# A fused attention and expert kernel: another order of loads, dots, far sums and turnings where its dense phase hands over to its expert phase

## The chip, the cores and the metric

One core of one Trainium2 chip runs the kernel in one launch. The metric is device time in microseconds (us): the median of 3 runs is 1411.21 us before the change (1410.98 to 1413.54). TensorE multiplies, VectorE and ScalarE do arithmetic on tiles, GpSimd (POOL) does some arithmetic and issues indirect DMAs, and SyncE (SP) issues most DMAs. Each engine works through its own queue in order and waits there for semaphores.

## The reference

All in float32, 4608 tokens of 512 elements:

```
kv = einsum('bhsd,bhse->bhde', k, v);  out = einsum('bhsd,bhde->bhse', q, kv)
x  = out / sqrt(mean(out*out, -1) + 1e-6) * g_norm        # 8 heads of 64 side by side: 512
h  = x @ w_in;  x = (max(h,0) + alpha*min(h,0)) @ w_out   # dense block, 512 -> 2048 -> 512
logits = x @ w_gate + modality_bias[modality_id]          # 8 experts
e_idx = argmax(logits);  gate_w = softmax(logits)[e_idx]
out[e_idx == e] = gate_w * (max(x[e_idx == e] @ w1[e], 0) @ w2[e])   # 512 -> 1024 -> 512
```

## The kernel before, in words

**First phase.** Twelve chunks (c) of 384 tokens. For each the attention of the next chunk is made beside the dense block of this one, which runs over 16 blocks (s) of 128 hidden elements: `first` (12 matmuls), then `second` (9 matmuls) of the block before. Numbers are split into a high and a low fp32r part, so each product is three matmuls. The dense weights lie in the tile `W`, 2048 columns per block. When a chunk is done, `y_out` copies its three tiles of 128 tokens (t) out of PSUM, `dots` makes the 24 logit columns per tile on VectorE, `choose`, `weigh`, `count` and `place` give expert, gate and a place in a bucket of that expert, and `scatter` writes the rows to the buffer `xb` in HBM. Beside this SyncE moves the experts' weights, split in parts, to `wsp` in HBM.

**Second phase.** 41 tiles (i) of 128 rows, each of one expert, sorted by expert; two slots in `W`, each with the 8 MB of one expert in two halves of 4 MB: the first half for `layer1` (24 matmuls), the second for `layer2` (24 matmuls). The expert with the most rows so far (the leader) comes first, since its first tiles are full before the last chunk is routed. Per tile: `load_rows` reads the rows from `xb` (four DMAs and a small one for gate and token number), `turn_rows` turns them and splits them (xhi, xlo), `layer1` with a ReLU (hh), `turn_h` turns and splits the result (hth, htl), `layer2` into PSUM (y2), a scaling and an indirect DMA to the output. Tiles 0 to 2 (`i < PLAIN`) are turned by TensorE through PSUM (4 transposes for rows, 8 for hh) and evicted by ScalarE and VectorE; later ones are turned by VectorE.

**Change of phase.** While the last chunk is still to be routed, TensorE already works on tiles 0 and 1 of the leader. The logits of the last chunk are divided: `dots` 0 to 7 and 16 to 21 (tiles t = 0 and 2 of the chunk, read straight from PSUM) on VectorE, and ten far ones, `far_mul` on GpSimd and `far_add` (a sum along the row) on ScalarE through two buffers. After `place`, `padding` writes eight blocks of empty rows (the ends of the buckets) to `xb`, `table` makes the lists that say which tile belongs to which expert, and from tile 4 on rows come from these lists.

**What sets the order.** It is written out by hand (`manual_schedule`): each engine gets its instructions in the order of the code, and semaphores are put between them. SyncE's DMAs take eight semaphores in turn; a DMA whose semaphore still belongs to one that has not landed waits for it. In `load_expert` SyncE waits for each half to land (L591) before its next instruction; and the first half of expert 0 and of expert 1 waits until the rows loaded last have landed (L589). PSUM tiles `y` (three banks) serve the last chunk's sums, then `turned` and y2; the pools opened at L941 to L943 take over the other banks. Two engines that read one PSUM bank are put one behind the other: `y_out(c, 0)` on ScalarE waits for the `dots` of that bank.

Of the kernel before, what the change touches and what calls it, by code (L numbers as in the profile page):

```python
# [8 lines left out]
F32 = mybir.dt.float32  # L9
# [5 lines left out]
ALU = mybir.AluOpType  # L15
# [4 lines left out]
NTOK = 4608  # L20
D = 512
S = 576
E = 8
# [4 lines left out]
BUCKET = 4736  # L28
NIT = 43
MAIN = 41  # L30
# [14 lines left out]
def fused(ctx: ExitStack, tc, qT, kv, g2, wmoe, alpha, wgate, bias, modality, w12, out):  # L45
# [58 lines left out]
    def other(n=512):  # L104
        return (pools[1] if pools else ps_a).tile([128, n], F32, tag="a", name="a")
# [289 lines left out]
    def y_out(c, t):  # L395
        if t == 1:
            lg_t[c] = one.tile([128, 3, E], F32, tag="lg", name="lg")
            yb_t[c] = [three.tile([128, ROW], F32, tag="yrow", name="yrow") for _ in range(3)]
        y = yb_t[c][t][:, 0:D]
        if t == 0 and c < NCH - 1:  # L400
            V.tensor_copy(y, y_t[c][t])
        else:
            A.copy(y, y_t[c][t])

    def dots(c, lo, hi):
        for i in range(lo, hi):
            t, e = divmod(i, E)
            y = y_t[c][t] if c == NCH - 1 else yb_t[c][t][:, 0:D]
            V.tensor_tensor_reduce(junk, y, wg_sb[:, e, :], 1.0, 0.0, ALU.mult, ALU.add, lg_t[c][:, t, e:e + 1])  # L409
# [72 lines left out]
    def padding():  # L482

        pi = one.tile([1, E], I32, name="pi")
        V.tensor_copy(pi, base[0:1, :])
        for e in range(E):
            r = SP.value_load(pi[0:1, e:e + 1], min_val=e * BUCKET, max_val=e * BUCKET + NTOK)
            i = SP.dma_start(xb[ds(r, 128)], pad)
            tc.declare_no_dep(i.ins, group="rows", reason="rows that no token has")
            if e:  # L490
                tc.declare_no_dep(i.ins, group="pads", reason="rows apart")
            tc.add_to_no_dep_group("pads", i.ins)
# [18 lines left out]
    def table():  # L511
# [62 lines left out]
        V.tensor_copy(ts[:, 1, :], ids[:, 0:E])  # L574
        yield

    def load_expert(j, halves=(0, 1)):
        tab = tab_0[0:1, 0:1] if j == 0 else tab_sp[0:1, E + j:E + j + 1]
        eid = SP.value_load(tab, min_val=0, max_val=E - 1)
        if j:  # L580
            thr = SP.value_load(tab_sp[0:1, j:j + 1], min_val=1, max_val=MAIN + 1)
        for half in halves:
            if j:
                SP.wait_ge(sem_2 if half else sem_1, thr)
            o = half * (SLOT // 2)
            at = (j & 1) * SLOT + o
            d = SP.dma_start(W[:, at:at + SLOT // 2].bitcast(F32), wsp[ds(eid, 1), :, o:o + SLOT // 2].rearrange("a p c -> p (a c)"))
            tc.add_to_no_dep_group("experts", d.ins)
            if j < 2 and half == 0:  # L589
                tc.add_manual_dep(d.ins, row_dma[0], data, reason="the first rows go first")  # L590
            s = SP.sem_inc(sem_w, 1)  # L591
            tc.add_manual_dep(s.ins, d.ins.name, data, reason="the weights are in")


    rows, x2, hh, ht, regs, row_dma = {}, {}, {}, {}, {}, []
# [19 lines left out]

    order = lambda t: t.rearrange("p (c a j) -> p c a j", c=4, a=4)

    def turned(x):
        ps = ps_y.tile([128, D], F32, tag="y", name="turned") if pools else other()
        for k in range(4):  # L620
            PE.transpose(ps[:, k * 128:(k + 1) * 128], x[:, k * 128:(k + 1) * 128], ident)
        return ps

    def turn_rows(i):

        x = rows.pop(i)
        o = (i % 3) * 512
        hi = xhi.rearrange("p a b -> p (a b)")[:, o:o + 512]
        lo = xlo.rearrange("p a b -> p (a b)")[:, o:o + 512]
        flat = x.rearrange("p a b -> p (a b)")  # L630
        if i < PLAIN:
            ps = turned(flat)
            A.copy(hi, ps)
            V.tensor_tensor(lo, ps, hi.bitcast(F32), ALU.subtract)
            x2[i] = hi, lo
            return
        V.transpose(flat, flat)
        x = x.rearrange("p a (c j) -> p c a j", c=4)
        A.copy(order(hi), x)
        V.tensor_tensor(order(lo), x, order(hi).bitcast(F32), ALU.subtract)  # L640
        x2[i] = hi, lo
# [114 lines left out]
    with tc.manual_schedule():  # L756
# [74 lines left out]
        for c in range(NCH):  # L831
# [3 lines left out]
            for s in range(NFB):  # L835
# [61 lines left out]
                if c > 0:  # L897
                    if s < 8:
                        dots(c - 1, 3 * s, 3 * s + 3)
                    if s == 7:  # L900
                        choose(c - 1)
                    if s == 8:
                        count(c - 1)
                        weigh(c - 1)
                    if s == 9:
                        place(c - 1)
                        if nxt == NCH:
                            leader()
                            scatter(c - 1, range(3))
                    if nxt < NCH and 9 <= s < 12:  # L910
                        scatter(c - 1, [s - 9])
                    if nxt == NCH and s == 11:
                        for i in range(3):
                            load_rows(i)
                        load_expert(0)
                elif edge:
                    pre_load(0)
                    SP.dma_start(wg_sb.rearrange("p a b -> p (a b)"), wgate.rearrange("a b -> (a b)").partition_broadcast(128))
                    G.memset(pad, 0.0)
                    G.memset(pad[:, D + 1:D + 2].bitcast(I32), OOB)  # L920
                    for j in range(8):
                        SP.dma_start(xb[E * BUCKET + j * 128:E * BUCKET + (j + 1) * 128], pad)
# [22 lines left out]
        add = lambda *js: [far_add(c, j) for j in js]  # L945
        far_mul(c, 0)
        far_mul(c, 1)
        add(0)
        dots(c, 0, 4)
        layer1(0, lambda: add(1, 2))  # L950
        turn_rows(2)
        load_rows(3)
        dots(c, 4, 8)
        y_out(c, 0)
        add(3, 4)
        layer1(1, lambda: add(5, 6))
        turn_h(0)
        dots(c, 16, 22)
        add(7, 8, 9)
        choose(c)  # L960
        weigh(c)
        layer2(0, lambda: count(c))
        place(c)
        scatter(c, range(3))
        padding()
        steps = table()
        next(steps)
        turn_h(1)
        next(steps)
        load_rows(4)  # L970
        load_rows(5)
        next(steps)
        for j in range(1, E):
            load_expert(j)
        for i in range(2, MAIN):
            if PLAIN < i + 1 < MAIN:
                turn_rows(i + 1)
            layer1(i)
            if i + 1 == PLAIN:
                turn_rows(i + 1)  # L980
            if 2 < i < MAIN - 3:
                load_rows(i + 3)
            if i == 3:
                _, words[:] = nc.values_load_multi_w_load_instructions(
                    tab_pe[0:1, 0:6], engines=[PE.engine], min_val=0, max_val=8 ** 8 - 1)
            if i == 8:
                items = nc.values_load(tab_pe[0:1, 6:7], min_val=0, max_val=NIT)
            layer2(i - 1)
            turn_h(i)
# [52 lines left out]
```

## Time and profile before

| | |
|---|---|
| median of 3 runs | 1411.21 us (1410.98 to 1413.54) |
| the profiled execution | 1413.03 us, of which the span is 1411.4 us |
| busy in the span | TensorE matmul 1365.8 us (97%), VectorE 1033.0 (73%), GpSimd 654.5 (46%), ScalarE 524.6 (37%) |
| granted TensorE clock, mean | 0.992 |

The span is what the engines' records cover; 1.6 us of the execution lie outside it. Times in the rows are us from the span's start. The first phase ends on TensorE at about 930 us; all of the change lies between about 911 us and 990 us.

### The profile page before, as it was taken

To read this page: it belongs to the slowest core of one execution; us is meant where nothing else is said; L and a number is where in the kernel's file an instruction comes from. 1 tells how busy PE (TensorE), PEld (TensorE's weight loads), DVE (VectorE), ACT (ScalarE), POOL (GpSimd) and SP (SyncE) were. 2 spreads that over 40 slices of the span, in tenths; PEclk is the share of its full clock that TensorE was granted. 3 is DMA by queue.
4 is the path that set the end of the run, shared out by engine and by line. 5 is a ranking of instruction groups with operands and counts; after the bars stand their busy time and mean duration, and the time that the engine had idled before them with its cause. 6 is when DMAs were issued, how large, how long until landed. Compare 5 with 4: busy or idle time off the path is not lost. (4 is left out here: it accounts for less than half of the span.)

```text
span 1411.4 us, 26831 instructions
## 1 busy us (share of the span) xinstructions
PE 1365.8 (97%) x8886; PEld 1160.9 (82%) x8886; DVE 1033.0 (73%) x2247; ACT 524.6 (37%) x1136; POOL 654.5 (46%) x641
## 2 busy tenths in 40 slices
PE   8889999999999999999999999979999999999997
PEld 7778888788888888888888888867888888888886
DVE  6999887777877687967887888737666666666663
ACT  4673323232322323232323232133445544445442
POOL 2665645455645464645555564532333333333321
PEclk9999999999999999999999999999999999999999
DMA  8854645454545554455645252464711161537784
GB/s 281 273 195 135 212 138 191 144 192 134 180 168 191 169 190 158 157 191 168 214 141 200 91 194 84 153 256 135 275 53 48 46 269 58 194 142 286 296 327 177
DMA packets 88950, 250.71 MB, mean 178 GB/s; under 512 B 19245, under 2 KB 39213, under 8 KB 86640
## 3 DMA queue, kind: packets, MB, share of 16 engines
q1 hardware_dynamic: 77056, 220.83, 45.0%
q0 software_dynamic: 11760, 28.14, 6.1%
q8 instruction: 78, 1.28, 0.4%
q14 instruction: 56, 0.46, 0.1%
HBM read 158.69 MB, written 91.54 MB: 177 GB/s over the span
## 5 line engine op out<-in xcount | busy, mean ns | idle before, releaser
L361 PE MATMUL h<-xhi,W 128*128 128x384 f32 x1536 | 429.7, 340 | 1.3 <-POOL W L185 0.7
L375 POOL TENSOR_TENSOR glo<-gg,ghi 128x384 fp32r<-128x384 f32 x192 | 225.8, 1177 | 388.7 <-ACT ghi L373 366.7
L389 PE MATMUL y<-W,ghi 128*128 128x512 f32 x1152 | 307.9, 402 | 24.1 <-ACT ghi L373 22.4
L361 PEld LDWEIGHTS h<-xhi,W 128*128 128x128 f32 x1536 | 281.7, 188 | 12.1 <-ACT xhi L350 1.4
L389 PEld LDWEIGHTS y<-W,ghi 128*128 128x128 f32 x1152 | 211.7, 189 | 74.9 <-ACT ghi L373 37.6
L361 PE MATMUL h<-xlo,W 128*128 128x384 f32 x768 | 259.3, 338 | 0.0
L409 DVE CUSTOM_DVE_ANT_0 junk<-yrow,wg_sb 128x512 f32<-128x512 f32 x264 | 244.4, 926 | 6.7
L645 PE MATMUL h<-W,xhi 128*128 (+1 forms) x656 | 207.5, 397 | 4.0 <-DMA W<-wsp 4.0
L645 PE MATMUL y<-W,hth 128*128 (+1 forms) x656 | 205.0, 394 | 5.4 <-DVE htl L697 5.0
L373 ACT CAST ghi<-gg 128x384 fp32r<-128x384 f32 x192 | 98.2, 512 | 267.9 <-DVE gg L369 201.0
L215 POOL TENSOR_TENSOR raw<-raw 128x512 f32<-128x512 f32 x128 | 197.1, 1540 | 0.5
L368 DVE TENSOR_SCALAR gg<-h,alpha_sb 128x384 f32<-128x384 f32 x176 | 107.5, 611 | 115.6 <-PE h L361 112.1
L211 ACT CAST raw<-raw 128x512 fp32r<-128x512 f32 x128 | 79.6, 622 | 279.2 <-DMA raw<-in_w_dram 166.2
L722 POOL DMA_INDIRECT out_dram<-kvbd,tail x41 | 43.6, 1063 | 282.6 <-ACT kvbd L720 240.9
L389 PE MATMUL y<-W,glo 128*128 128x512 f32 x576 | 168.4, 401 | 0.0
L645 PEld LDWEIGHTS y<-W,hth 128*128 128x128 f32 x656 | 124.2, 190 | 34.2 <-DVE htl L697 5.3
L645 PEld LDWEIGHTS h<-W,xhi 128*128 128x128 f32 x656 | 123.7, 189 | 34.0 <-DVE lg L409 4.3
L361 PEld LDWEIGHTS h<-xlo,W 128*128 128x128 f32 x768 | 144.2, 188 | 6.9 <-DVE xlo L351 0.2
L389 PEld LDWEIGHTS y<-W,glo 128*128 128x128 f32 x576 | 107.4, 190 | 30.9 <-POOL glo L375 6.3
L645 PE MATMUL y<-W,htl 128*128 (+1 forms) x328 | 130.4, 398 | 0.0
L645 PE MATMUL h<-W,xlo 128*128 (+1 forms) x328 | 130.1, 397 | 0.0
L682 DVE TENSOR_SCALAR hh<-h 32x256 f32<-32x256 f32 x296 | 123.3, 416 | 4.6
(204 smaller groups left out, 1469.5 us busy)
## 6 DMA issues: line engine op xcount, KB each, us to landing
wsp<-raw SPq DMA_DIRECT2D x128, 512.0 KB
W<-wsp SPq DMA_DIRECT2D x16, 4096.0 KB
raw<-in_w_dram SPq DMA_DIRECT2D x128, 256.0 KB
kvt<-in_kv_dram SPq DMA_DIRECT2D x30, 512.0 KB
xs<-xb POOLq DMA_DIRECT2D x140, 64.0 KB
raw<-in_wmoe_dram SPq DMA_DIRECT2D x17, 512.0 KB
qT<-in_qT_dram SPq DMA_DIRECT2D x11, 768.0 KB
wg_sb<-in_wmoe_dram SPq DMA_DIRECT2D x15, 512.0 KB
```

What stands on the lines that cost most here:

```text
L211: A.copy(sp_t[n][:, 0:512].bitcast(F32R), sp_t[n][:, 512:1024])
L215: G.tensor_tensor(lo, lo, hi, ALU.subtract)
L361: PE.matmul(ps, w_at(fb, part)[:, k * 128:(k + 1) * 128], x[:, k, :], start=(i == 0), stop=(i == 11))
L368: V.tensor_scalar(gg, ps, 0.0, alpha_sb[:, fb:fb + 1], ALU.min, ALU.mult)
L373: A.copy(ghi, gg)
L375: G.tensor_tensor(glo, gg, ghi.bitcast(F32), ALU.subtract)
L389: PE.matmul(y_t[c][t], a[:, t * 128:(t + 1) * 128], w, start=(fb == i == 0), stop=(fb == NFB - 1 and i == 2))
L409: V.tensor_tensor_reduce(junk, y, wg_sb[:, e, :], 1.0, 0.0, ALU.mult, ALU.add, lg_t[c][:, t, e:e + 1])
L645: m = PE.matmul(ps, a, w, start=start, stop=stop)
L682: m = V.tensor_scalar(to, of, 0.0, None, ALU.max) if mine else A.activation(to, of, AF.Relu)
L722: d = G.indirect_dma_start(out=out, out_offset=IndirectOffsetOnAxis(ap=tail[:, i, 1:2].bitcast(I32), axis=0), in_=y, in_offset=None, bound ...
```

## The change

At block s = 11 of the last chunk SyncE's queue gets the rows of tile 0, the first half of the leader's weights, the rows of tiles 1 and 2, then the second half. SyncE no longer waits behind the first half of expert 0: its semaphore for both is counted up after the second. The wait for the rows loaded last (L589) stays for expert 1 only. The transposes of tile 1 go to the PSUM bank `spare`. `dots` 0 to 7 come in one run ahead of `layer1(0)`, four far sums between the halves of `layer1(0)`, then `y_out(c, 0)`, which stood behind the second half of the dots. `turn_h(0)` moves into `layer1(1)`, between its two halves of 12 matmuls; `turn_h(1)` goes ahead of the scatter and the tables; `turn_rows(3)` ahead of the last part of the tables; `turn_h(2)` into `layer2(1)`, behind its 18th matmul. `padding` loads the eight ends into registers with one load ahead of the eight writes.

On SyncE, from the rows of tile 2 to the rows of tile 3, before (`xs` are rows, `tail` the small DMA, TENSOR_LOAD and ISA fetch an address; each waits for the semaphores named):

```order
L614 DMA tail<-xb 128x2 [waits DMAHW0_49]
L579 TENSOR_LOAD tab_111
L579 ISA x2
L587 ISA
L587 DMA W<-wsp 128x8192 [waits DMAHW7_49,DMAHW1_49,PE_49]
L587 ISA [waits DMAHW1_49]
L587 DMA W<-wsp 128x8192 [waits DMAHW2_49,PE_49]
L604 TENSOR_LOAD tab_111 [waits DMAHW2_49]
```

Now, from the rows of tile 0 into the rows of tile 1, and then from the rows of tile 2 on:

```order
L623 DMA tail<-xb 128x2 [waits DMAHW6_49]
L584 TENSOR_LOAD tab_111
L584 ISA x2
L592 ISA
L592 DMA W<-wsp 128x8192 [waits DMAHW1_49,DMAHW7_49,DMAHW0_49,PE_49]
L613 TENSOR_LOAD tab_111
L613 ISA x2
L621 ISA
L621 DMA xs<-xb 128x4x32
```

```order
L621 DMA xs<-xb 128x4x32 [waits DMAHW7_49]
L621 ISA
L621 DMA xs<-xb 128x4x32 [waits DMAHW0_49]
L623 ISA
L623 DMA tail<-xb 128x2 [waits DMAHW1_49]
L584 TENSOR_LOAD tab_111
L584 ISA x2
L592 ISA
L592 DMA W<-wsp 128x8192 [waits DMAHW2_49,PE_49]
L613 TENSOR_LOAD tab_111 [waits DMAHW7_49,DMAHW2_49]
```

The first half stands two tiles of rows earlier; the third piece of rows of tile 2 now waits for its landing (semaphore DMAHW7), the second half waits for the third piece of tile 1's rows (DMAHW2), and the wait for both halves stands ahead of the rows of tile 3.

On TensorE, around the end of `layer1(1)` (h_9889), before:

```order
L645 MATMUL h_9889<-W,xhi 128x512 x2
L645 MATMUL h_9889<-W,xlo 128x512
L621 MATMUL turned<-ident,hh 128x128 x8
L645 MATMUL y_9972<-W,hth 128x512 x2
L645 MATMUL y_9972<-W,htl 128x512
```

and now, in the middle of `layer1(1)` (h_9901) and on to `layer2(0)` (y_9980):

```order
L654 MATMUL h_9901<-W,xlo 128x512
L630 MATMUL turned<-ident,hh 128x128 x8
L654 MATMUL h_9901<-W,xhi 128x512 x2
L654 MATMUL h_9901<-W,xlo 128x512
L654 MATMUL h_9901<-W,xhi 128x512 x2
L654 MATMUL h_9901<-W,xlo 128x512
L654 MATMUL h_9901<-W,xhi 128x512 x2
L654 MATMUL h_9901<-W,xlo 128x512
L654 MATMUL h_9901<-W,xhi 128x512 x2
L654 MATMUL h_9901<-W,xlo 128x512
L654 MATMUL y_9980<-W,hth 128x512 x2
```

The eight transposes of tile 0's hidden rows no longer stand directly ahead of `layer2(0)`: twelve matmuls of `layer1(1)` lie between.

On ScalarE, from the last far sum ahead of `layer1(0)`'s ReLU on (kvbd are the far products, hh the ReLUs, hth the turned and rounded result), before:

```order
L418 ACTIVATE kvbd_100,lg<-kvbd_100 128x512
L677 ACTIVATE hh<-h_9826 128x4x4x32 x2
L633 CAST xhi<-turned 128x512
L403 COPY yrow<-y 128x512
L418 ACTIVATE kvbd_101,lg<-kvbd_101 128x512
L418 ACTIVATE kvbd_100,lg<-kvbd_100 128x512
L418 ACTIVATE kvbd_101,lg<-kvbd_101 128x512
L418 ACTIVATE kvbd_100,lg<-kvbd_100 128x512
L677 ACTIVATE hh<-h_9889 128x4x4x32 x2
L696 CAST hth<-turned 128x512 x2
```

and now:

```order
L418 ACTIVATE kvbd_101,lg<-kvbd_101 128x512
L686 ACTIVATE hh<-h_9836 128x4x4x32 x2
L403 COPY yrow<-y 128x512
L642 CAST xhi<-turned 128x512
L418 ACTIVATE kvbd_100,lg<-kvbd_100 128x512
L418 ACTIVATE kvbd_101,lg<-kvbd_101 128x512
L705 CAST hth<-turned 128x512 x2
L418 ACTIVATE kvbd_100,lg<-kvbd_100 128x512
L418 ACTIVATE kvbd_101,lg<-kvbd_101 128x512
L686 ACTIVATE hh<-h_9901 128x4x4x32 x2
```

Two far sums, not four and a ReLU, stand between the rounding of tile 2's rows (xhi) and that of tile 0's hidden rows (hth).

The diff, cut to its core:

```diff
         V.tensor_copy(pi, base[0:1, :])
+        _, ends = nc.values_load_multi_w_load_instructions(pi, engines=[SP.engine], min_val=0, max_val=E * BUCKET)
         for e in range(E):
-            r = SP.value_load(pi[0:1, e:e + 1], min_val=e * BUCKET, max_val=e * BUCKET + NTOK)
+            r = SP.alloc_register(f"end{e}")
+            SP.reg_alu(r, ends[e], 0, ALU.add)
+            r = SP.snap(r, min_val=e * BUCKET, max_val=e * BUCKET + NTOK)
...
-            if j < 2 and half == 0:
+            if j == 1 and half == 0:
                 tc.add_manual_dep(d.ins, row_dma[0], data, reason="the first rows go first")
-            s = SP.sem_inc(sem_w, 1)
-            tc.add_manual_dep(s.ins, d.ins.name, data, reason="the weights are in")
+            landed.append(d.ins.name)
+            if j == half == 0:
+                continue
+            while landed:
+                s = SP.sem_inc(sem_w, 1)
+                tc.add_manual_dep(s.ins, landed.pop(0), data, reason="the weights are in")
...
-            ps = turned(flat)
+            ps = turned(flat, None if pools else spare if i else other())
...
-                        for i in range(3):
-                            load_rows(i)
-                        load_expert(0)
+                        load_rows(0)
+                        load_expert(0, (0,))
+                        load_rows(1)
+                        load_rows(2)
+                        load_expert(0, (1,))
...
-        add(0)
-        dots(c, 0, 4)
-        layer1(0, lambda: add(1, 2))
+        dots(c, 0, 8)
+        layer1(0, lambda: add(0, 1, 2, 3))
+        y_out(c, 0)
         turn_rows(2)
         load_rows(3)
-        dots(c, 4, 8)
-        y_out(c, 0)
-        add(3, 4)
-        layer1(1, lambda: add(5, 6))
-        turn_h(0)
-        dots(c, 16, 22)
-        add(7, 8, 9)
+        dots(c, 16, 18)
+        add(4, 5)
+        layer1(1, lambda: [turn_h(0), add(6, 7)])
+        dots(c, 18, 22)
+        add(8, 9)
         choose(c)
         weigh(c)
-        layer2(0, lambda: count(c))
+        layer2(0)
+        count(c)
         place(c)
+        turn_h(1)
         scatter(c, range(3))
         padding()
         steps = table()
         next(steps)
-        turn_h(1)
         next(steps)
         load_rows(4)
         load_rows(5)
+        layer1(2)
+        turn_rows(3)
         next(steps)
         for j in range(1, E):
             load_expert(j)
-        for i in range(2, MAIN):
-            if PLAIN < i + 1 < MAIN:
+        layer2(1, lambda: turn_h(2))
+        for i in range(PLAIN, MAIN):
+            if i + 1 < MAIN:
                 turn_rows(i + 1)
             layer1(i)
-            if i + 1 == PLAIN:
-                turn_rows(i + 1)
```

## Rows read from the trace of the kernel before

**Rows 1.** The page, part 1: busy us, share of the span, instructions.
```profile
PE 1365.8 (97%) x8886; PEld 1160.9 (82%) x8886; DVE 1033.0 (73%) x2247; ACT 524.6 (37%) x1136; POOL 654.5 (46%) x641
```
**Rows 2.** Windows: us, busy by engine, granted clock, DMA share, GB/s.
```profile
115.50:123.50 8.00, 8.00 (x43) 7.46 (x43) 6.46 (x14) 2.63 (x5) 1.68 (x2) 1.00 1.02 294
...
915.60:918.60 3.00, 3.00 (x18) 2.78 (x17) 0.88 (x2) 0.00 (x0) 0.81 (x1) 1.00 0.68 91
...
954.50:960.00 5.50, 5.50 (x13) 4.35 (x14) 5.12 (x16) 1.60 (x6) 1.29 (x1) 0.50 0.00 0
...
970.00:1380.00 410.00, 410.00 (x1780) 333.29 (x1779) 271.44 (x528) 199.63 (x439) 137.99 (x212) 1.00 0.51 183
```
**Rows 3.** Timeline of TensorE: start, us, line, out<-in, idle before and its releaser.
```profile
930.49 0.60 PE L621 MATMUL a<-ident,xs 128*128 128x128 f32 x4
935.13 0.70 PE L645 MATMUL h<-W,xhi 128*128 128x512 f32 x2 [4.05 <-DMA W<-wsp]
...
942.35 0.60 PE L621 MATMUL turned<-ident,xs 128*128 128x128 f32 x4
942.71 0.71 PE L645 MATMUL h<-W,xhi 128*128 128x512 f32 x2
...
948.39 1.04 PE L621 MATMUL turned<-ident,hh 128*128 128x128 f32 x8
954.43 1.22 PE L645 MATMUL y<-W,hth 128*128 128x512 f32 x2 [5.01 <-DVE htl L697]
...
962.83 1.03 PE L621 MATMUL turned<-ident,hh 128*128 128x128 f32 x8
...
969.27 0.62 PE L645 MATMUL y<-W,hth 128*128 128x512 f32 x2
...
974.77 1.03 PE L621 MATMUL turned<-ident,hh 128*128 128x128 f32 x8
...
992.35 0.62 PE L645 MATMUL y<-W,hth 128*128 128x512 f32 x2
```
**Rows 4.** Timeline of SyncE's DMA issues: start, us of the group, line, out<-in.
```profile
114.70 4.47 SPq L922 DMA_DIRECT2D xb<-pad  x8
...
914.65 2.10 SPq L612 DMA_DIRECT2D xs<-xb  x4
...
922.85 12.78 SPq L587 DMA_DIRECT2D W<-wsp  x2
...
964.54 9.80 SPq L488 DMA_DIRECT2D xb<-pad  x8
978.24 1.96 SPq L612 DMA_DIRECT2D xs<-xb  x4
```
**Rows 5.** Waits of SyncE's queue, 905 to 985 us: total, times, longest.
```profile
SPq L591 <- DMA W<-wsp: 23.6, 2, 11.8
```
**Rows 6.** Timeline of VectorE.
```profile
932.05 0.69 DVE L634 TENSOR_TENSOR xlo<-a,xhi 128x512 fp32r<-128x512 f32 x1 [2.16 <-ACT xhi L633]
...
944.76 0.68 DVE L409 CUSTOM_DVE_ANT_0 junk<-y,wg_sb 128x512 f32<-128x512 f32 x1
...
974.84 0.69 DVE L640 TENSOR_TENSOR xlo<-xs,xhi 128x512 fp32r<-128x512 f32 x1 [0.69 <-ACT xhi L639]
...
982.62 0.71 DVE L637 STREAM_TRANSPOSE xs<-xs 128x512 f32<-128x512 f32 x1 [5.16 <-DMA xs<-xb]
...
989.55 0.69 DVE L703 TENSOR_TENSOR htl<-hh,hth 128x512 fp32r<-128x512 f32 x1 [0.69 <-ACT hth L702]
```
**Rows 7.** Timeline of ScalarE.
```profile
932.41 0.63 ACT L418 ACTIVATE kvbd<-kvbd 128x512 f32<-128x512 f32 x1 [0.40 <-POOL kvbd L413]
...
947.69 0.59 ACT L403 COPY yrow<-y 128x512 f32<-128x512 f32 x1 [3.56 <-DVE lg L409]
...
953.07 1.07 ACT L696 CAST hth<-turned 128x512 fp32r<-128x512 f32 x2
```
**Rows 8.** Timeline of GpSimd.
```profile
931.12 6.21 POOL L413 TENSOR_TENSOR kvbd<-yrow,wg_sb 128x512 f32<-128x512 f32 x5 [2.07 <-ACT yrow L403]
```

More of the change, by code (lines that the diff above doesn't have):

```diff
@@ L575, in table @@
         yield
+    landed = []
     def load_expert(j, halves=(0, 1)):
@@ L616, in fused, with turned @@
     order = lambda t: t.rearrange("p (c a j) -> p c a j", c=4, a=4)
-    def turned(x):
-        ps = ps_y.tile([128, D], F32, tag="y", name="turned") if pools else other()
+    def turned(x, to=None):
+        ps = ps_y.tile([128, D], F32, tag="y", name="turned") if pools else to
         for k in range(4):
@@ L974, in fused @@
             load_expert(j)
-        for i in range(2, MAIN):
-            if PLAIN < i + 1 < MAIN:
+        layer2(1, lambda: turn_h(2))
+        for i in range(PLAIN, MAIN):
+            if i + 1 < MAIN:
                 turn_rows(i + 1)
             layer1(i)
-            if i + 1 == PLAIN:
-                turn_rows(i + 1)
-            if 2 < i < MAIN - 3:
+            if i < MAIN - 3:
                 load_rows(i + 3)
-            if i == 3:
+            if i == PLAIN:
                 _, words[:] = nc.values_load_multi_w_load_instructions(
```

## The prediction

> **What bounds the kernel now.** I read the page's busy line first: TensorE's matmuls fill 97% of the span [rows 1]. Then the windows: from 970 to 1380 us TensorE is busy for all 410.00 us at a granted clock of 1.00 [rows 2], so nothing can be won there. What an edit at the change of phase is worth is therefore the idle and the slow time of TensorE between the last sum of the dense phase (930.49 us) and the steady tiles. Its timeline [rows 3] shows two gaps there: 4.05 us ahead of `layer1(0)`, ended by the landing of the weights' first half, and 5.01 us ahead of `layer2(0)`, ended by VectorE's low part of the turned hidden rows. Behind each gap the same work takes longer. `layer1(0)` needs 942.35 - 935.13 = 7.22 us and `layer1(1)`, the same 24 matmuls, 948.39 - 942.71 = 5.68: 1.54 lost. `layer2(0)` needs 962.83 - 954.43 = 8.40 and `layer2(1)` 974.77 - 969.27 = 5.50: 2.90 lost. The reason stands in the windows: after the gap the granted clock is 0.50, the lower of its two levels (1.2 GHz), from 954.5 to 960.0 [rows 2]. All four together, 4.05 + 1.54 + 5.01 + 2.90 = 13.5 us, is the most that this change can win, unless waits elsewhere go too.
>
> **The loads on SyncE.** Before, the first half is issued at 922.85 [rows 4], behind the rows of three tiles; a half lands 11.8 us after its issue [rows 5]. Now it stands where the rows of tile 1 stood, at 914.65 [rows 4], so it lands at 926.5. TensorE wants it at 930.49 plus 0.36 for four transposes (942.71 - 942.35, [rows 3]) = 930.85: the 4.05 us go, and with them the slow stretch behind them. What is late next is a choice of two. `layer1(0)` had a second wait: its PSUM tile takes over banks that the transposes of tile 1 used, which VectorE reads until 932.05 + 0.69 = 932.7 [rows 6]. With those transposes in `spare` it waits for tile 0's alone; without that edit 1.9 us of the gap would have stayed. The other is the rows of tile 1, which TensorE turns at 930.49. They now stand behind 4 MB in the same queue. The trace of before shows no small DMA behind a big one at this place, so I bound it: the rows of one tile keep the DMA engines busy for 3.00 us at a share of 0.68 [rows 2], 2.0 us of full work, which gives 926.5 + 2.0 = 928.5 at best; from the first issue of a tile's rows to their use by VectorE it took 982.62 - 978.24 = 4.4 us [rows 4, 6], which gives 930.9 at worst. The wait is 0 to 0.4 us; I take 0, as the address work of these DMAs is done by then.
>
> The Trainium skill ("DMA: Bandwidth & Descriptors", Queues, rings and completion order) says that on each DMA engine descriptors are consumed in ring order. That speaks against the edit: by the rule the rows come only after the weights, the 0 to 0.4 us above; if the engines served both side by side, the rows would be there by 920 and the half 2 to 4 us later, still no wait. No row here decides between the two, and the sum takes 0 by both.
>
> The second half: the third piece of tile 2's rows waits for the first half (926.5), and two more DMAs (2.10 / 4 = 0.53 us each, [rows 4]) and an address load follow. Eight writes with a load each took 9.80 us and eight without 4.47 [rows 4], so a load costs (9.80 - 4.47) / 7 = 0.76. That is 926.5 + 1.6 + 0.8 = 928.9, or up to 931.3 if tile 1's third piece is late. The half lands at 940.7 to 943.1; `layer2(0)` will want it at 943.6 (below). Nothing is charged.
>
> **Dots, far sums and turnings.** TensorE: `layer1(0)` 930.85 to 936.53, four transposes to 936.89, half of `layer1(1)` to 939.73, the first four transposes of `turn_h(0)` to 940.09. The other four need a PSUM bank that tile 2's rows give back. That chain: eight dots at (947.69 - 944.76) / 4 = 0.73 [rows 6, 7] from 932.7 end at 938.5; `y_out(0)` 0.59 and the rounding of tile 2, 1.07 / 2 [rows 7], reach 939.7; the low part, 0.69 [rows 6], 940.4. So TensorE stands 0.3 us in the middle of `layer1(1)`: the one new wait that I charge. From both sides it is 0 (dots as fast as four were) to 1.3 us (ScalarE one sum later). Far sums: a product takes 6.21 / 5 = 1.24 on GpSimd [rows 8], so the fourth is there at 936.1, its sum (0.63, [rows 7], and reading it out) at 936.9, two ReLUs at 938.0, before `y_out(0)` can start. After the rounding two sums (941.0) and the two roundings of hth, 1.07 (942.1); VectorE has two dots till 941.9 and the low parts at 942.6 and 943.3. `layer2(0)` starts at 940.4 + 0.36 + 2.84 = 943.6, a microsecond after the first low part. Before, four sums that waited for their products and a ReLU stood ahead of hth, at 953.07 [rows 7]. So the 5.01 us go as well, and the slow stretch. This cover of 1.0 us is thin: whatever delays the chain further goes straight into TensorE.
>
> **Ends and tables.** `layer2(0)` ends at 949.1. The counting matmuls now stand behind it, not six matmuls ahead of its end; that leaves TensorE's work the same. Before, the first end was written at 964.54 [rows 4], 3.1 us after the counting (962.83 less a quarter of 5.50). Now VectorE has two low parts of `turn_h(1)` ahead, 1.4, and one load of eight registers stands ahead of the first write; that load is not shown, between 0 and 7 x 0.76 = 5.3 us more; I take 1.2, nearer to one load. First end at 949.1 + 3.1 + 1.4 + 1.2 = 954.8. Eight in a row, issued from 114.70, kept the DMA engines full until 123.50 [rows 2, 4]: 8.8 us, so 963.6. With about 0.6 to the rows' issue and 4.4 to their use, tile 4's rows reach VectorE at 968.6. They are needed 989.55 + 0.69 - 982.62 = 7.6 us [rows 6] ahead of `layer2(3)`, which started at 992.35 [rows 3] and now starts at 979.2: by 971.5. Cover 2.9 us, no charge; at the old pace of 978.24 - 964.54 = 13.7 us [rows 4] it would be 971.7, a wait of 0.2, and with the load at its dearest some 2 us. For tile 3, VectorE took from the counting (961.4) to 974.84 + 0.69 [rows 6] 14.1 us with the last part of the tables, which now comes later: at most 949.1 + 14.1 = 963.2 against 962.4, when `layer1(3)` starts; without that part no wait.
>
> **The sum.** 13.5 - 0.3 = 13.2 us less: the span 1411.4 becomes 1398.2, the profiled execution of 1413.03 us (1.6 outside the span) 1399.8. That execution stands 1.8 over the median of 1411.21, so the median becomes 1398.0 us.
>
> **Rivals.**
> - The waits come back in part (chance 0.18). Covers are 1.0 us (hth), 0.5 to 2.9 (second half), 2.9 (tile 4's rows). For it: three queues run into one another, and a gap of 4 us also halves the clock. Against: each cover is reckoned with the dearer row. If the second half lands at 945.4 and the chain is 1 us later, 2.8 us and half of a slow stretch, 1.5, come back: 1402.3. All upper bounds together make 1404.
> - Only the weights' gap goes (0.07): ScalarE still has hth late, as its sums wait for GpSimd. Then 4.05 + 1.54 are won: 1405.6. Against: the products are ready 2.4 us before ScalarE asks for them.
> - Slower (0.03). VectorE takes its queue in order, and ahead of the ReLUs of tile 3 stands the turning of tile 4, which waits for the ends and the last rows scattered. Each microsecond past 971.5 costs one. It decides from 971.5 + 13.2 + 2.8 = 987.5: the eight writes would have to take 28 us instead of 8.8. At 30 they give 16.6 of the win back by the wait and some 1.5 to 3 by the clock, about 1415. Against: that window ran with full DMA engines already [rows 2].
> - The change doesn't do what it says (0.04): the first half still stands behind something in its list of semaphores and the second gap passes to a like wait; 1411. The built order names no semaphore of rows for it.
>
> **Numbers.** Forecast 0.68, at 1398.0, its own range 1396.5 to 1400.5. The measurement tells about 0.2%, 2.8 us, from no change. Faster than that: 0.68 + 0.18 + 0.07 = 0.93; within: 0.04; slower: 0.03. The range runs from the whole 13.5 us and a run a microsecond faster, 1396.5, to the upper bounds of the first rival, 1404.
>
> **What would show it.** Right: no wait of TensorE for the weights, `layer1(0)` at once after the transposes, 5.7 us long; a gap of some 0.3 us among the transposes in `layer1(1)`; none ahead of `layer2(0)`; clock 1.00 from 930 on; `layer2(3)` at about 979. Wrong: a wait ahead of tile 1's transposes (the queue's order), ahead of `layer2(0)` (half or hth), or VectorE idle for tile 4's rows beyond 971.5.

## The result and the profile after

The changed kernel takes 1398.99 us (median of 4 runs, 1397.0 to 1400.29) against 1411.61 us (4 runs): a ratio of 0.991, interval 0.9896 to 0.9923. The profiled execution took 1399.09 us, its span is 1397.5. The forecast was 1398.0 us.

I read the waits of TensorE from 900 to 1000 us first (engine, line, what ended the wait: us in total, times, longest). Both waits of before [rows 3] are gone, and one that was not there has come:

```profile
PE y L654 <- DMA W<-wsp: 1.4, 1, 1.4
```

TensorE's timeline places it (start, us, line, out<-in, idle before and its releaser):

```profile
928.35 0.60 PE L630 MATMUL spare<-ident,xs 128*128 128x128 f32 x4
928.70 0.71 PE L654 MATMUL h<-W,xhi 128*128 128x512 f32 x2
...
934.36 0.60 PE L630 MATMUL turned<-ident,xs 128*128 128x128 f32 x4
...
937.59 1.30 PE L630 MATMUL turned<-ident,hh 128*128 128x128 f32 x8
...
943.13 0.71 PE L654 MATMUL y<-W,hth 128*128 128x512 f32 x2 [1.44 <-DMA W<-wsp]
...
948.81 1.07 PE L630 MATMUL turned<-ident,hh 128*128 128x128 f32 x8
...
978.40 0.62 PE L654 MATMUL y<-W,hth 128*128 128x512 f32 x2
```

`layer1(0)` starts at once behind the transposes of tile 1 and takes 934.36 - 928.70 = 5.66 us, not 7.22. The eight transposes inside `layer1(1)` take 1.30 us, not the 1.04 of [rows 3]: the small gap among them. The 1.44 us stand ahead of `layer2(0)`, for the second half of the weights. From 926 to 1370 us nothing is left of the slow clock; windows (us, busy by engine, granted clock, DMA share, GB/s):

```profile
926.00:950.00 24.00, 22.52 (x113) 18.03 (x112) 15.77 (x55) 14.21 (x36) 13.70 (x12) 1.00 0.58 198
950.00:980.00 30.00, 30.00 (x135) 24.48 (x134) 20.20 (x66) 9.63 (x20) 11.55 (x16) 1.00 0.70 226
970.00:1370.00 400.00, 400.00 (x1732) 324.95 (x1732) 268.71 (x513) 200.01 (x441) 133.81 (x206) 1.00 0.50 183
```

SyncE's timeline answers to [rows 4]:

```profile
909.16 2.16 SPq L621 DMA_DIRECT2D xs<-xb  x4
911.50 0.36 SPq L623 DMA_DIRECT2D tail<-xb  x1
912.81 0.35 SPq L592 DMA_DIRECT2D W<-wsp  x1
913.95 9.39 SPq L621 DMA_DIRECT2D xs<-xb  x4
923.52 2.93 SPq L623 DMA_DIRECT2D tail<-xb  x1
927.25 2.08 SPq L621 DMA_DIRECT2D xs<-xb  x4
929.52 0.36 SPq L623 DMA_DIRECT2D tail<-xb  x1
930.74 0.35 SPq L592 DMA_DIRECT2D W<-wsp  x1
...
956.20 4.60 SPq L491 DMA_DIRECT2D xb<-pad  x8
965.60 1.95 SPq L621 DMA_DIRECT2D xs<-xb  x4
```

The rows of tile 1, right behind the first half, take 9.39 us to issue where 2.1 were usual, and their small DMA 2.93 instead of 0.36. The rows of tile 2 and the second half come only after that.

**A measure apart from the first phase.** The transposes of tile 1 start at 928.35 here and at 930.49 before [rows 3], though nothing was changed ahead of them on TensorE. Those 2.1 us lie earlier than any instruction that was changed: SyncE's last store of the experts' weights stands at 900.23 here and at 902.38 before. Over the fourteen profiled executions of this study that start lies between 924.8 and 930.5. So I compare the *rest*: the span less that start. Before it is 1411.4 - 930.49 = 480.9 us, now 1397.5 - 928.35 = 469.15. The change is worth 11.8 us in the rest. The medians differ by 12.6, which agrees within the spread of the first phase. The rest itself repeats well: the same kernel once more (e11 below) has 468.6, which is 0.6 less, and 0.55 of that is its shorter wait for the second half (0.89 us).

### The profile page after: what moved, and what is told of

Same layout as the page of the kernel before. It is cut to its first block, busy times and chain, and to the rows that moved or that the text cites. A ratio compares the mean times of both kernels' runs of the same rounds, so it can differ in the third digit from the quotient of the medians.

```text
span 1397.5 us, 26825 instructions
## 1 busy us (share of the span) xinstructions
PE 1360.4 (97%) x8886; PEld 1157.0 (83%) x8886; DVE 1038.2 (74%) x2247; ACT 524.6 (38%) x1136; POOL 653.9 (47%) x641
```

## The experiments

Each kernel is the changed one with the edit shown. The columns are the median, the span of the profiled execution, the start of tile 1's transposes in it, and the rest, which is their difference.

| kernel | median us | span | start | rest |
|---|---|---|---|---|
| before | 1411.61 | 1411.4 | 930.49 | 480.9 |
| changed | 1398.99 | 1397.5 | 928.35 | 469.2 |
| e1_loads_old | 1405.29 | 1403.7 | 930.19 | 473.5 |
| e2_orders_old | 1405.32 | 1403.7 | 928.53 | 475.2 |
| e3_no_spare | 1399.43 | 1397.4 | 928.26 | 469.1 |
| e4_ends_singly | 1397.49 | 1394.9 | 926.68 | 468.2 |
| e5_rows1_first | 1400.13 | 1398.5 | 929.31 | 469.2 |
| e6_rows2_last | 1399.01 | 1396.7 | 928.41 | 468.3 |
| e7_turn_h0_after | 1400.18 | 1399.8 | 929.93 | 469.9 |
| e8_far_old | 1399.47 | 1397.3 | 926.12 | 471.2 |
| e9_weights_first | 1397.32 | 1391.9 | 924.77 | 467.1 |
| e10_weights_first_only | 1397.08 | 1395.5 | 927.31 | 468.2 |
| e11_again | 1398.73 | 1396.1 | 927.55 | 468.6 |
| e12_rows2_after | 1397.51 | 1395.1 | 927.87 | 467.2 |

The medians are of 4 to 6 runs, each beside runs of the kernel before, whose medians there were 1410.7 to 1412.0 us; the interval of each ratio to the kernel before is about 0.0015 wide to either side, 2 us. Where a verdict hangs on less, the rest and the waits decide it.

### The old loads (e1_loads_old)

```
-load_rows(0); load_expert(0, (0,)); load_rows(1); load_rows(2); load_expert(0, (1,))
+load_rows(0); load_rows(1); load_rows(2); load_expert(0)      # and its old waits
```

> The changed kernel with the old loads alone: rows of three tiles, then both halves of expert 0's weights, the first after the rows have landed. Theory S (each wait has a price of its own, and the prices add): the first half is issued about 11.5 us after rows 0, as before, so TensorE waits 4 us for it ahead of layer1(0), and the new wait of 1.44 us ahead of layer2(0) goes, since everything there comes 4 us later. With the clock at 1.00: 1399.0 + 4.0 - 1.4 = 1401.6; with layer1(0) at the low clock as in the kernel before (+1.5): 1403.1. Theory O (the new orders are what counts, they would hide a late half too): 1399 to 1400, no TensorE wait over 1 us.

TensorE's timeline and windows of this run:

```profile
930.19 0.60 PE L624 MATMUL spare<-ident,xs 128*128 128x128 f32 x4
934.58 1.19 PE L648 MATMUL h<-W,xhi 128*128 128x512 f32 x2 [3.79 <-DVE lg L409]
...
942.64 0.60 PE L624 MATMUL turned<-ident,xs 128*128 128x128 f32 x4
```

```profile
934.50:940.00 5.50, 5.42 (x13) 4.34 (x14) 3.51 (x12) 1.45 (x4) 3.77 (x4) 0.51 0.84 316
```

The wait is back, 3.79 us. The releaser that the row names is the wrong one of several: VectorE's eight dots run on past it until 938.2 us, while the first half, issued at 922.15, had its last packet at 934.01, and TensorE starts at 934.58. The low clock is back too, 0.51, and `layer1(0)` takes 942.64 - 934.58 = 8.06 us, 2.4 more than at 1.00. No wait is left ahead of `layer2(0)`. 3.79 + 2.40 - 1.44 - 0.26 (that gap is gone too) = 4.5, and the rest is 4.35 longer. The median is 6.3 us above that of the changed kernel; 1.84 of that lie ahead of the transposes in the profiled execution (930.19 against 928.35). Theory S holds, with a low clock dearer than I took; theory O is out.

### The old orders (e2_orders_old)

```
-dots(c, 0, 8); layer1(0, lambda: add(0, 1, 2, 3)); y_out(c, 0); ...
+add(0); dots(c, 0, 4); layer1(0, lambda: add(1, 2)); ...    # and all that follows, to the loop over tiles
```

> The changed kernel with the old orders of dots, far sums, turnings and layers; loads, the bank of tile 1's turning and the ends as changed. Theory S: the wait of 5.0 us for htl ahead of layer2(0) is back and with it the low clock behind it (+2.9), the wait of 1.44 for weights is hidden in it: 1399.0 + 5.0 + 2.9 - 1.4 - 0.3 = 1405.2. Rival P (the chain of dots on VectorE runs at its own pace, so that TensorE, which now comes 5.6 us sooner to layer2(0), waits 5.6 us longer there): a wait of about 10 us, 1409 to 1411, and the new loads alone are worth nearly nothing.

TensorE's timeline, and the window behind the gap:

```profile
940.58 1.04 PE L630 MATMUL turned<-ident,hh 128*128 128x128 f32 x8
946.63 1.22 PE L654 MATMUL y<-W,hth 128*128 128x512 f32 x2 [5.02 <-DVE htl L706]
```

```profile
946.60:952.00 5.40, 5.37 (x13) 4.21 (x14) 5.05 (x16) 1.70 (x6) 1.29 (x1) 0.50 0.01 0
```

The wait of 5.0 us is back with its low clock: 1405.32 us where theory S gave 1405.2, and 6.0 us in the rest where it gave 6.2. `layer2(0)` starts 946.63 - 928.53 = 18.1 us behind the transposes, and 954.43 - 930.49 = 23.9 in the kernel before: it came sooner by 5.8 us, about what the loads won for TensorE, and the wait stayed the same. So rival P is out: the chain that ends in htl moves with TensorE's first matmuls. The two parts add up. In e1 and in e2 the wait of 1.44 us for the second half is hidden, so the loads are worth 4.35 + 1.44 and the orders 6.0 + 1.44; the changed kernel still has the 1.44, and 5.8 + 7.4 - 1.44 gives the 11.8 of both together.

### Tile 1 in the old bank, and ends read singly (e3_no_spare, e4_ends_singly)

```
-ps = turned(flat, None if pools else spare if i else other())
+ps = turned(flat, None if pools else other())
```

> The changed kernel with tile 1's transposes written to a bank of the old rotation instead of spare. Theory S: layer1(0) starts 1.9 us later, since it waits for that bank until xlo of tile 1 has read it; the wait for the second half of weights ahead of layer2(0) shrinks from 1.44 to 0 in return: 1399.0 + 1.9 - 1.4 = 1399.5, with a wait of 1.5 to 2 us on TensorE ahead of layer1(0). Rival: the bank is free in time, no wait, 1399.0. Rival: the gap brings the low clock for layer1(0) as the 4.05 us did: 1401.

TensorE's timeline:

```profile
930.57 0.72 PE L654 MATMUL h<-W,xhi 128*128 128x512 f32 x2 [1.71 <-DVE xlo L643]
```

The wait is there, 1.71 us (1.9 in the prediction), put down to the low part of tile 1. The other one is gone, and the rest is that of the changed kernel. `spare` is worth nothing while the second half is late. It should be worth up to 1.7 us once it isn't, but no run shows that.

```
-_, ends = nc.values_load_multi_w_load_instructions(pi, engines=[SP.engine], ...)
+r = SP.value_load(pi[0:1, e:e + 1], ...)                    # one for each of the eight, ahead of its write
```

> The changed kernel with the eight ends read one register at a time, each ahead of its DMA, as before. Theory S: the first end is written sooner, the last one some 3 us later than now (9.8 us for the eight against 4.6); tile 4's rows, which wait for all of them, come 3 us later, and their users have 7 us in hand: no TensorE wait, 1399.0. Rival: rows 4 and 5 and expert 1's weights behind them on SyncE's queue come late, and TensorE waits up to 2 us in layer1(3) or layer1(4): 1400 to 1401.

SyncE's timeline:

```profile
950.87 9.34 SPq L488 DMA_DIRECT2D xb<-pad  x8
963.30 1.98 SPq L618 DMA_DIRECT2D xs<-xb  x4
```

Against the transposes the first end goes out 24.2 us behind them, in the changed kernel 27.85; the eight take 9.34 us and 4.60; and tile 4's rows are issued 36.6 and 37.25 behind. Less each run's wait for the second half (0.50 here, which the row puts down to a dot, though the half's last packet passed at 940.04, 0.48 us ahead of TensorE's start; 1.44 there) that is 36.1 and 35.8. What the one load saves between the writes it costs ahead of the first. TensorE waits for neither. The rest is 0.95 us shorter, which is what the wait for the second half is shorter by: this part of the change is worth nothing.

### What makes the second half late (e5_rows1_first, e6_rows2_last)

```
-load_rows(0); load_expert(0, (0,)); load_rows(1); load_rows(2); load_expert(0, (1,))
+load_rows(0); load_rows(1); load_expert(0, (0,)); load_rows(2); load_expert(0, (1,))
```

> Order of SyncE's queue: rows 0, rows 1, first half, rows 2, second half. Theory Q (what stands behind 2 MB on SyncE's queue is issued only once most of the 2 MB is through, so the second half comes late by one tile's issue, 3.5 us, that can go ahead of the weights instead): rows 1 take 2.1 us to issue and not 9.4, rows 2 stand in their place; the first half is issued 3.5 us later and lands 0 to 0.4 us ahead of its use, the second lands 1 to 1.4 us sooner than in the changed kernel against tile 1's transposes: the wait of 1.44 us ahead of layer2(0) falls to 0 to 0.3, a new one of 0 to 0.4 may come ahead of layer1(0). From tile 1's transposes to the end of the span 467.8 to 468.6 against 469.15; median 1397.5 to 1398.5. Rival L (the 9.4 us are the wait for a lane or for rows 1's own data): rows 1 stand as long here, ahead of the weights, and the first half comes 7 us late: 1405.

SyncE's timeline, then the one wait of TensorE:

```profile
913.55 2.11 SPq L621 DMA_DIRECT2D xs<-xb  x4
915.87 0.34 SPq L623 DMA_DIRECT2D tail<-xb  x1
917.41 0.36 SPq L592 DMA_DIRECT2D W<-wsp  x1
918.54 2.64 SPq L621 DMA_DIRECT2D xs<-xb  x4
921.38 9.77 SPq L623 DMA_DIRECT2D tail<-xb  x1
932.01 0.35 SPq L592 DMA_DIRECT2D W<-wsp  x1
```

```profile
931.49 0.70 PE L654 MATMUL h<-W,xhi 128*128 128x512 f32 x2 [1.58 <-DMA W<-wsp]
```

The rows of tile 1 are issued in 2.11 us, and it is now tile 2's small DMA that stands, 9.77 us, until 931.15, just behind the last packet of the half (930.80). So theory Q holds and rival L is out (a lane is one of the eight semaphores that SyncE's DMAs take in turn): of the rows that come right behind these 4 MB on SyncE's queue, one DMA stands until the 4 MB are nearly or wholly through. (Some expectations call a half 2 MB; it is 4.) The wait ahead of `layer2(0)` is gone. But the first half took 931.49 - 917.41 = 14.1 us, where I had reckoned with 11.8 to 12.3, and is 1.58 us late: nothing is won. All its packets but the last had passed at 929.50; why one DMA engine was behind isn't shown.

```
-load_rows(0); load_expert(0, (0,)); load_rows(1); load_rows(2); load_expert(0, (1,))
+load_rows(0); load_rows(1); load_expert(0, (0, 1)); load_rows(2)
-layer2(0)
+layer2(0, lambda: turn_rows(2))             # turn_rows(2) no longer behind layer1(0)
```

> Rows 0, rows 1, both halves, rows 2; tile 2's rows are turned inside layer2(0) and not after layer1(0). Theory Q: the second half stands 12 to 13 us in its issue and lands within 24 us of the first one's issue, 1 to 2 us ahead of its use; no wait ahead of layer2(0), and the 0.26 us in the turning of hidden tile 0 goes, since tile 2's rows no longer hold a bank there: 469.15 - 1.44 - 0.26 = 467.4; median 1397.3. Rival: tile 2's rows now land behind both halves, at the end of layer1(1) or later, and hold up layer2(0), in whose stream their transposes stand: a wait of 1 us or more there, 1399 or more.

TensorE's timeline:

```profile
929.87 0.70 PE L654 MATMUL h<-W,xhi 128*128 128x512 f32 x2 [0.86 <-DMA W<-wsp]
```

No wait ahead of `layer2(0)` and none in the turning of hidden tile 0, as forecast, but here too the first half is late, by 0.86 us, 13.5 after its issue. The rest is 0.85 us shorter; the median shows nothing.

### Which of the orders (e7_turn_h0_after, e8_far_old)

```
-layer1(1, lambda: [turn_h(0), add(6, 7)])
+layer1(1, lambda: add(6, 7)); turn_h(0)
```

> The changed kernel with hidden tile 0 turned after layer1(1) and not inside it. Theory S: htl comes 2.5 us later against layer1(1)'s end, layer2(0) starts when it would by its weights, at 14.8 us after tile 1's transposes: no change, 1399.0, with the wait now put down to htl. Rival: the chain through ScalarE costs more there, 2 to 5 us and the low clock behind it: 1401 to 1406; then this place and not the order of dots and far sums is what took away the 5 us.

TensorE's timeline, and the window behind the gap:

```profile
945.46 0.73 PE L654 MATMUL y<-W,hth 128*128 128x512 f32 x2 [2.44 <-DVE htl L706]
```

```profile
946.00:952.00 6.00, 6.00 (x34) 4.87 (x32) 5.38 (x29) 1.34 (x5) 0.00 (x0) 1.00 0.18 36
```

The wait is 2.44 us and put down to htl, 1.0 longer than the one it replaces; the rest is 0.75 longer, and the clock stays at 1.00. Theory S is right but for those 0.75 us, and the rival is out.

```
-dots(c, 0, 8); layer1(0, lambda: add(0, 1, 2, 3)); y_out(c, 0); turn_rows(2); load_rows(3)
-dots(c, 16, 18); add(4, 5); layer1(1, lambda: [turn_h(0), add(6, 7)]); dots(c, 18, 22); add(8, 9)
+add(0); dots(c, 0, 4); layer1(0, lambda: add(1, 2)); turn_rows(2); load_rows(3)
+dots(c, 4, 8); y_out(c, 0); add(3, 4); layer1(1, lambda: [turn_h(0), add(5, 6)]); dots(c, 16, 22); add(7, 8, 9)
```

> The changed kernel with the old order of dots and far sums alone; hidden tile 0 is still turned inside layer1(1). Theory F (the chain of dots, y_out and ScalarE's adds sets when htl is ready, wherever TensorE turns): layer2(0) starts 17 to 18 us after tile 1's transposes, a wait of 3 to 5 us with the low clock behind it: 1402 to 1405. Rival (the place of the turning counts, the order of dots does not): 1399 to 1400.

TensorE's timeline, and the window behind the gap:

```profile
935.37 0.60 PE L630 MATMUL turned<-ident,hh 128*128 128x128 f32 x4
938.11 0.66 PE L630 MATMUL turned<-ident,hh 128*128 128x128 f32 x4 [2.14 <-ACT yrow L403]
...
942.94 0.62 PE L654 MATMUL y<-W,hth 128*128 128x512 f32 x2
```

```profile
938.00:943.00 5.00, 4.89 (x17) 3.98 (x18) 3.13 (x7) 3.61 (x11) 4.24 (x4) 0.66 0.32 101
```

`layer2(0)` starts 942.94 - 926.12 = 16.8 us behind the transposes (14.8 in the changed kernel), by 2.14 us of waiting among the transposes of `turn_h(0)`, whose bank waits for the copy of `y_out`, and by a clock of 0.66 behind that. The rest is 2.05 us longer. The median shows 0.5 of it, which its spread allows; it lies where the rival said (1399 to 1400) and below the 1402 of theory F. By the trace neither is right: the order does count, but at half of F's price. Alone, then, the turning's place is worth 0.75 us and the order of dots and sums 2.05, each beside a late second half that hides up to 1.44 us more; with all orders old (e2) it is 6.0. Either of the two already takes away most of that. The later orders (`turn_h(1)`, `turn_rows(3)`, `turn_h(2)` and the layers around the tables) were not taken back alone; in e2, where they are old too, TensorE has no second wait from 900 to 1000 us.

### Towards a faster version (e9 to e12)

```
now: -load_rows(0); load_expert(0, (0,)); load_rows(1); load_rows(2); load_expert(0, (1,))
e9:  +load_expert(0, (0,)); load_rows(0); load_rows(1); load_expert(0, (1,)); load_rows(2)   # turn_rows(2) as in e6
e10: +load_expert(0, (0,)); load_rows(0); load_rows(1); load_rows(2); load_expert(0, (1,))
e11: the changed kernel
e12: +load_rows(0); load_expert(0, (0,)); load_rows(1); load_expert(0, (1,)); load_rows(2)   # turn_rows(2) as in e6
```

> Order of SyncE's queue: first half, rows 0, rows 1, second half, rows 2; tile 2's rows are turned inside layer2(0). The table from which the expert is read is written 5 us before rows 0 are issued in the changed kernel, so the first half can go out 6 us sooner than there (at -22 us against tile 1's transposes, not -15.5). Theory Q: it has landed by -9 us, rows 0 and 1 stand behind it and are issued by -2 us, rows 0 in time for their turning at -2.5, rows 1 at 0; the second half goes out by -3 us and lands by +9, its use is at +13.3. No TensorE wait in the phase: 469.15 - 1.44 - 0.26 = 467.4, median 1397.3. Rival: rows 0 or rows 1, now behind 2 MB on the ring, come late and TensorE waits 1 us or more ahead of their turning: 1399 or more. Rival: the first half waits for something else (the last expert weights being stored) and goes out no sooner: 1400.

> Order of SyncE's queue: first half, rows 0, rows 1, rows 2, second half; the turning of tile 2 as in the changed kernel. Theory Q: the second half goes out at about -1 us against tile 1's transposes and lands by +11.5, its use is at +13.3: no wait for weights, 469.15 - 1.44 = 467.7, median 1397.5. Rivals as for the run before.

> The changed kernel once more, on the same chip as the two others, for their medians: 1399.0; 469 from tile 1's transposes to the end of the span, with a wait of 0.5 to 1.5 us for the second half of the weights.

> Order of SyncE's queue: rows 0, first half, rows 1, second half, rows 2; tile 2's rows are turned inside layer2(0). It keeps the changed kernel's place of the first half, behind the scatter's rows, and spares the second half the issue of rows 2 (3.5 us). Theory Q: the second half goes out 3.4 us sooner, 1 us ahead of tile 1's transposes or at them, and lands by +11 to +12, its use is at +13.3; rows 2 stand behind it, land at about +12 and are turned at +17; the 0.26 us in the turning of hidden tile 0 goes too: 469.15 - 1.44 - 0.26 = 467.4 (467.3 was measured with the first half ahead of rows 0), median 1397.3, no TensorE wait in the phase. Rival: rows 1, which are issued piecemeal behind the first half, are now followed at once by the second half, and their last packets share the engines with it: up to 1 us of wait ahead of tile 1's transposes, 1398 to 1399.

In e9 TensorE doesn't stand once: the window from 920 to 950 us (TensorE's busy time comes after the length) shows it, and the rest is 467.1, forecast 467.4.

```profile
920.00:950.00 30.00, 30.00 (x148) 24.58 (x146) 22.05 (x80) 15.58 (x38) 17.66 (x15) 1.00 0.60 196
```

In e10 only a part of it came: a wait of 0.53 us for the second half stays. SyncE's timeline tells why, then its longest wait, and GpSimd's scatter in the view of the DMA issues (issues, median us to landing):

```profile
904.09 0.37 SPq L592 DMA_DIRECT2D W<-wsp  x1
917.92 2.12 SPq L621 DMA_DIRECT2D xs<-xb  x4
...
929.03 0.35 SPq L592 DMA_DIRECT2D W<-wsp  x1
```

```profile
SPq L621 <- DMA xb<-yrow,pos: 12.6, 1, 12.6
```

```profile
xb<-yrow,pos POOLq DMA_INDIRECT x3, 8.2
```

The first half went out 23 us ahead of the transposes, as expected, but into the scatter that writes the rows to `xb`. That takes 8.2 us to land, and SyncE waits 12.6 us for it (3.8 in the changed kernel, same view; 12.8 in e9). So the rows come late, and the second half goes out 1.7 us behind the transposes and not 1 ahead. e12 leaves the first half behind the rows of tile 0, and the second half goes out 1.6 us ahead of the transposes (SyncE's timeline, then the window):

```profile
926.23 0.34 SPq L592 DMA_DIRECT2D W<-wsp  x1
```

```profile
915.00:950.00 35.00, 35.00 (x174) 29.39 (x173) 21.78 (x69) 16.57 (x39) 17.76 (x15) 1.00 0.70 254
```

There is no TensorE wait in the phase, and the rest is 467.2, as forecast. e9, e10 and e12 have medians of 1397.1 to 1397.5, e11 and the changed kernel 1398.7 and 1399.0. Against the kernel before, e9 stands at 0.9902 (0.9886 to 0.9917), e11 beside it at 0.9911 (0.9894 to 0.9929): the intervals overlap, so the medians alone don't tell the two apart. The waits and the rest do: 467.1 and 467.2 us against 468.6 and 469.2, 1.4 to 2.1 us less.

## Why the prediction was right, and the step that failed

**The sum.** 13.5 us were the two gaps and the slow stretches behind them. All went: no gap, clock 1.00, 5.66 us for `layer1(0)`. Charged were 0.3 for the gap among the transposes of `turn_h(0)`; it measures 1.30 - 1.04 = 0.26. With the 1.44 us that were not charged, 13.50 - 0.26 - 1.44 = 11.8, which is the difference of the rests. So the forecast of 13.2 is 1.4 us too large. That the medians fell by 12.6 brings it nearer, but those 0.8 us are the spread of the first phase and no merit of the prediction; the first phase of this execution, 2.1 us shorter, is no part of the change.

**The step that failed: "The half lands at 940.7 to 943.1; `layer2(0)` will want it at 943.6. Nothing is charged."** Use: 13.1 us behind the transposes were forecast, 943.13 - 1.44 - 928.35 = 13.3 measured. Issue: -1.6 to 0.8 forecast, 930.74 - 928.35 = 2.4 measured. I had let SyncE run on until a semaphore stops it in the third piece of tile 2's rows, with two more DMAs to go. Instead it stands one tile earlier, while it issues the third DMA of tile 1's rows. The semaphore of that DMA is the one that the first DMA of tile 0's rows had taken, eight DMAs ahead, and that one had long landed; so I take it that room on the queue keeps SyncE there, though no run shows the room itself. SyncE's timeline:

```profile
915.64 7.07 SPq L621 DMA_DIRECT2D xs<-xb  x1
```

So a whole tile of rows, 3.5 us with its address load, is left between the landing of the first half and the second half's issue. Besides, 11.8 was SyncE's wait alone; from its issue to TensorE's start the half takes 943.13 - 930.74 = 12.39 us, as before (935.13 - 922.85 = 12.28 [rows 3, 4]). The 1.44 us are the 2.39 - 0.81 = 1.58 by which the issue is later than the latest forecast and the 12.39 - 11.8 = 0.59, less the 0.5 us that were left at worst and the 0.23 by which TensorE asks later. This cover was one of those that the first rival named, and it ends where that rival said, at a part of its price. How late it is differs from run to run: 1.44, 0.89 in e11, 0.50 in e4.

**Order on the queue.** The packet records show the rows of tile 1 passing from 924.15 to 927.35 us. Two of their four DMAs had been issued by 915.13, but no packet of theirs passed before the first DMA engine was through with the weights (924.14); the records don't name the engines. That is the ring order of the rule which the prediction weighed (the Trainium skill, "DMA: Bandwidth & Descriptors", Queues, rings and completion order); the trace agrees. They were there 1.0 us ahead of their use, so the 0 that was taken is right. The first half was no longer 4 us early: its last packet passed at 926.13, 13.3 us after the issue and not 11.8. All but that one had passed at 924.66; one DMA engine was behind. In e11, the same kernel, it took 12.0.

**The chain of dots.** ScalarE copied out at once, and the low parts came where they were forecast: VectorE's first was to be ready 12.1 us behind the transposes, and is at 939.43 + 0.64 - 928.35 = 11.7.

ScalarE's timeline, then VectorE's:

```profile
936.38 0.59 ACT L403 COPY yrow<-y 128x512 f32<-128x512 f32 x1 [0.55 <-DVE lg L409]
...
938.58 1.07 ACT L705 CAST hth<-turned 128x512 fp32r<-128x512 f32 x2
```

```profile
939.43 1.28 DVE L706 TENSOR_TENSOR htl<-turned,hth 128x512 fp32r<-128x512 f32 x2
```

**Edits whose worth was mis-stated.** The 1.9 us of `spare` measured 1.7 as a wait, but took nothing off the rest, as the 1.44 and the 0.26 went in return (e3). The load of eight registers was taken at 1.2 us more than one load, from 0 to 5.3; against e4 it is (27.85 - 1.44) - (24.2 - 0.5) = 2.7. The load itself takes 0.55 us (0.28 in e4); the rest passes with the register operations behind it, until 955.8. Tile 4's rows came to VectorE 41.4 us behind the transposes, not 38.1; its timeline:

```profile
969.75 0.71 DVE L646 STREAM_TRANSPOSE xs<-xs 128x512 f32<-128x512 f32 x1 [5.72 <-DMA xs<-xb]
...
976.68 0.69 DVE L712 TENSOR_TENSOR htl<-hh,hth 128x512 fp32r<-128x512 f32 x1 [0.69 <-ACT hth L711]
```

The cover held, but by 978.40 - 977.37 = 1.0 us and not 2.9.

**Rivals.** The gaps came back in part, 1.44 of 2.8 us, all of it at the second half and without the clock. That the weights' gap alone goes is e2's case, and there it costs what was said (1405.6 forecast, 1405.32 measured for that part alone). Nothing speaks for the slower one. Its sum has a slip: with 30 us for the eight writes tile 4's rows come 21.2 us later, which is 18.3 past the cover of 2.9 and not 16.6, and the time some 1418 us; no chance hangs on it. The last rival is out as well: the first half was issued at 912.81, ahead of the rows of tiles 1 and 2.

## What to carry to other kernels

Price a gap of the matrix engine with the slow stretch behind it, and sum the gaps of the stage: here that gave the size of a change of many parts to 1.4 us in 11.8. Where a big transfer goes out earlier, ask what stands behind it on the issuing queue. Between two big transfers put only what is wanted before the second one, and what is wanted later behind both: that took the last wait away in e9 and e12, where the rows of tile 2 moved there. An early big transfer also delays the small ones of other queues that run at the time: look at what they feed before moving it up.

## What the runs showed of the hardware

- **A queue stands behind a big transfer.** Rows of one tile are issued in 2.1 us; right behind 4 MB the third DMA of them stood 7.07 us, until 922.71, when the weights' last packets were about to start (the first of these at 922.87), and the small one 2.93, until 926.45, just behind their end at 926.13. With another tile's rows ahead of the 4 MB only the small one stood, 9.77 us, and also until just behind the end (e5). The issue of the 4 MB took 0.35 us, and a second 4 MB directly behind the first did not stand (e6, 0.94 us for both).
- **Packets of two queues take turns.** With the first half in the scatter's way, the records show, from 905 us on, as many scatter packets (128, of 4112 bytes, 0.16 us each) as weights packets (128, of 32768 bytes, 1.21 us each), and the last scatter packet through at 917.3 us (e10); in the changed kernel, where the weights came later, it was through at 908.2. The rule of turns by packet between queues (the Trainium skill, "DMA: Bandwidth & Descriptors", Queues, rings and completion order) says the same.
- **Not each gap costs the clock.** Behind waits of 1.44, 1.71 and 2.44 us (after, e3, e7) the granted clock stayed at 1.00; behind 2.14 us (e8) it was 0.66 over the next 5 us, a mean of both levels, and behind 3.79 (e1) and 5.02 us (e2) 0.51 and 0.50, its lower level. What tells 2.14 from 2.44 wasn't tried.
